# Loads and gradient stores issued by SyncE instead of GpSimd, beside a long zero fill

## The chip, the cores and the metric

The kernel runs on one NeuronCore of a Trainium2 chip. The metric is device time in microseconds of one execution, as a median over runs. The engines are TensorE (PE), VectorE (DVE), ScalarE (ACT), GpSimd (POOL) and SyncE (SP). Transfers between the device's memory and the on-chip memory are issued by SP, ACT or POOL, each into a queue of its own, and are carried out by the core's 16 DMA engines.

## What is computed

One decode step of a transformer block for two sequences, forward and backward: layer norm, attention over the last 4096 positions of a key/value cache, a GELU-gated feed-forward layer, and the gradients of all inputs.

```python
B, Sq, D = 2, 1, 512
Hq, Hkv, Sk, Dh = 32, 8, 32768, 128
F = 1792
W = min(4096, max(256, Sk // 4))                       # 4096

def _A_ref(x, k_cache, v_cache, wq, wo):
    q = heads(x @ wq)
    k = jnp.repeat(k_cache[:, :, Sk - W:, :], rep, axis=1)
    v = jnp.repeat(v_cache[:, :, Sk - W:, :], rep, axis=1)
    p = softmax(einsum("bhqd,bhkd->bhqk", q, k) * Dh ** -0.5)
    return heads_back(einsum("bhqk,bhkd->bhqd", p, v)) @ wo

def _B_ref(x, w_gate, w_up, w_down):
    return (gelu(x @ w_gate) * (x @ w_up)) @ w_down

h  = x + _A_ref(layernorm(x), k_cache, v_cache, wq, wo)
h2 = h + _B_ref(layernorm(h), w_gate, w_up, w_down)
# outputs: h2, and the gradients of x, k_cache, v_cache, wq, wo, w_gate, w_up, w_down
```

All tensors are bfloat16. Two facts set the amount of data. The gradients of the two caches have the caches' full shape, 2 x 8 x 32768 x 128, though only the last 4096 positions differ from zero: the other 28672 positions of each of the 32 (tensor, sequence, head) regions must be written with zeros, 7.34 MB each and 234.9 MB in all. And the gradient at the 4096 positions is another 33.6 MB. The loads are the used parts of the caches (33.6 MB) and the weights.

## The kernel before

The on-chip memory is one large byte array `mem`, and `at(off, shape, ...)` gives a tile at a hand-picked offset, so several tensors use the same bytes in turn. A tile of K or V (`Kt[b, g]`, `Vt[b, g]`) is 1 MB: 128 partitions with 32 cache rows each, 8 KB per partition. Loads go by `load_k` (line 148) and `load_v` (line 152).

The program runs these stages: `attention(0)`, `middle(0)`, `score_grads(0)`, `attention(1)`, `middle(1)`, then `score_grads(1)` interleaved with the weight gradients, the gradient of the query projection, and last the gradients of the caches. `attention(b)` goes through the eight K/V heads g. Within it the order of PE, VectorE and ScalarE is written out by hand (`manual_schedule`), with the softmax steps of head g + 1 put between the products of head g. For SP and GpSimd the order is that of the program text all through.

`prefetch(b, g)` is called at the start of head g and issues what later heads need: in the first sequence K and V of head g + 3, then the output projection (g = 5), the gate weights (6), the up weights and the first two K of the second sequence (8); in the second sequence the V and K tiles, each as its place comes free. K has four places in the first sequence, and in the second some heads share a place, so a K load waits until the head that used it is done.

Zeros are written from a tile `zt` of 128 x 2048 bytes of zero. The transfer reads bytes and writes 4-byte elements, so that a row of 2048 bytes in becomes 8 KB out; casting transfers are issued by GpSimd (`zero_rows`, line 114). `zeros(n)` writes the next n columns, a column being 128 such rows or 1 MB, and there are 7 columns to a region. Where a whole region is started at once and its number is in `ZERO_PARTS`, it goes out as five to seven transfers with other numbers of rows, such as `(15, 18)`: 15 rows of 18 x 8 KB.

Before the change almost all transfers are in GpSimd's one queue, and the program text decides their order: a load, some zeros, a load, and so on. SP issues only x, the query weights, the first two K and V tiles, the down weights (twice) and x once more (line 138, before the weight gradients), and stores the gradient of x (line 857). `store` (line 795) writes the gradients of the output projection and of the feed-forward weights, line 873 those of the query weights, line 909 the 16 stores of the cache gradients of 2 MB each (`dKv`, `dVv`); zeros follow each of them. In the last stage VectorE and ScalarE evacuate the products of line 901 through `evac` (lines 91 and 93) into eight staging places, and each place can be used again when its store has landed.

Of the kernel before, what the change touches and what calls it, by code (L numbers as in the profile page):

```python
# [8 lines left out]
F32 = mybir.dt.float32  # L9
U8 = mybir.dt.uint8  # L10
U32 = mybir.dt.uint32
ACT = mybir.ActivationFunctionType
ALU = mybir.AluOpType
# [3 lines left out]
P = 128  # L17
B, D = 2, 512
# [6 lines left out]
F = 1792  # L25
NFR = F // P
NDR = D // P
NOR = (HQ * DH) // P
# [40 lines left out]
def kernel(ctx, tc, A_x, A_k_cache, A_v_cache, A_wq, A_wo, B_x, B_w_gate, B_w_up, B_w_down, grad_out,  # L69
                out_0, out_1, out_2, out_3, out_4, out_5, out_6, out_7, out_8):  # L70
    nc = tc.nc
# [24 lines left out]
    Kv = A_k_cache[:, :, Z:, :].rearrange("b g (p j) d -> p b g j d", p=P)  # L96
    Vv = A_v_cache[:, :, Z:, :].rearrange("b g (p j) d -> p b g j d", p=P)
# [3 lines left out]
    ZE = 2048  # L101
    zt = const.tile([P, ZE], U8)
    zero_regions = [o[b, g, 0:Z, :].rearrange("r d -> (r d)") for o in (out_2, out_3) for b in range(B) for g in range(HKV)]

    ZPK = Z * DH // 2 // ZE

    ZCOLS = ZPK // P
    ZERO_PARTS = {5: ((4, 1), (15, 2), (2, 2), (15, 18), (12, 1), (128, 4), (16, 4)), 15: ((4, 1), (15, 2), (2, 2), (15, 18), (12, 1), (128, 4), (16, 4)), 27: ((3, 16), (15, 2), (3, 4), (15, 18), (12, 2), (128, 4)), 6: ((6, 2), (1, 6), (9, 2), (12, 2), (4, 1), (128, 6), (16, 4)), 7: ((8, 2), (1, 6), (7, 2), (12, 2), (4, 1), (128, 6), (16, 4)), 14: ((9, 2), (1, 6), (6, 2), (12, 2), (4, 1), (128, 6), (16, 4)), 16: ((10, 2), (1, 6), (5, 2), (12, 2), (4, 1), (128, 6), (16, 4)), 17: ((12, 2), (1, 6), (3, 2), (12, 2), (4, 1), (128, 6), (16, 4)), 18: ((13, 2), (1, 6), (2, 2), (12, 2), (4, 1), (128, 6), (16, 4)), 19: ((14, 2), (1, 6), (1, 2), (12, 2), (4, 1), (128, 6), (16, 4))}
    TAIL_ZEROS = (1, 1, 1, 2, 2, 1, 1, 1, 2, 2, 1, 1, 1, 2, 2, 0)
    z_cols = [0]  # L110

    def zero_rows(dst, rows, n):
        src = zt[0:rows * (P // rows):P // rows, :]
        nc.gpsimd.dma_start(out=dst.rearrange("(p k e) -> p k e", p=rows, k=n),  # L114
                            in_=src.unsqueeze(1).to_broadcast([rows, n, ZE]))

    def zeros(n):
        while n:
            i, c = divmod(z_cols[0], ZCOLS)
            parts = ZERO_PARTS[i] if c == 0 and n >= ZCOLS and i in ZERO_PARTS else ((P, min(n, ZCOLS - c)),)  # L120
            done = c * P
            for rows, k in parts:
                zero_rows(zero_regions[i].bitcast(F32)[done * ZE:(done + rows * k) * ZE], rows, k)
                done += rows * k
            assert done % P == 0
            z_cols[0] += done // P - c
            n -= done // P - c

    dh2_x = at(OFF_XR, [98, D], BF16, "xr")
    dh2_bf, x_32, dh_bf = dh2_x[0:B, :], dh2_x[32:32 + B, :], dh2_x[64:64 + B, :]  # L130
# [10 lines left out]
    wq_sb = at(OFF_WQ, [P, NDR, HQ * DH], BF16, "wq")  # L141
    nc.sync.dma_start(out=wq_sb[:], in_=A_wq.rearrange("(p r) n -> p r n", r=NDR))
    load_rows(nc.scalar)
    Kt, Vt = {}, {}

    def load_k(b, g, eng=nc.gpsimd):
        Kt[b, g] = at(K_OFF[b][g], [P, NJ, DH], BF16, f"K{b}_{g}")
        eng.dma_start(out=Kt[b, g][:], in_=Kv[:, b, g, :, :])

    def load_v(b, g, eng=nc.gpsimd):  # L150
        Vt[b, g] = at(OFF_V + g * 8 * KIB, [P, NJ, DH], BF16, f"V{b}_{g}")
        eng.dma_start(out=Vt[b, g][:], in_=Vv[:, b, g, :, :])

    wo_sb = at(OFF_WO, [P, NOR, D], BF16, "wo")
    wg = at(OFF_WG, [P, NDR, F], BF16, "wg")
    wu = at(OFF_WU, [P, NDR, F], BF16, "wu")
# [5 lines left out]
        nc.sync.dma_start(out=t[:], in_=B_w_down.rearrange("(m r) n -> m r n", r=NFR))  # L162

    def load_wg():
        nc.gpsimd.dma_start(out=wg[:], in_=B_w_gate.rearrange("(p r) f -> p r f", r=NDR))

    def load_wu():
        nc.gpsimd.dma_start(out=wu[:], in_=B_w_up.rearrange("(p r) f -> p r f", r=NDR))

    ident_bf = const.tile([P, P], BF16)  # L170
    nc.gpsimd.memset(ident_bf[:], 0.0)
# [131 lines left out]
    def prefetch(b, g):  # L303
        if b == 0:
            if g == 0:
                load_k(0, 0, nc.sync)
                load_wd(OFF_WD0)
                for i in range(2):
                    load_v(0, i, nc.sync)
                    if i == 0:  # L310
                        load_k(0, 1, nc.sync)
                nc.gpsimd.tensor_scalar(out=zt[:], in0=Kt[0, 0][:, 0:ZE // 256, :].rearrange("p j d -> p (j d)").bitcast(U8),
                                        scalar1=0, scalar2=None, op0=ALU.mult)
                for i in range(2, 4):
                    load_k(0, i)
                    load_v(0, i)
                zeros(9)
            elif g + 3 < HKV:
                load_k(0, g + 3)
                zeros(2)  # L320
                load_v(0, g + 3)
                zeros(2)
            elif g == 5:
                nc.gpsimd.dma_start(out=wo_sb[:], in_=A_wo.rearrange("(p r) n -> p r n", r=NOR))
                zeros(0)
            elif g == 6:
                load_wg()
                zeros(6)
            elif g == HKV:
                load_wu()  # L330
                load_k(1, 0)
                load_k(1, 1)
                zeros(27)
        else:
            if g == 0:
                for i in range(5):
                    load_v(1, i)
                    zeros(1)
                for i in range(2, 5):
                    load_k(1, i)  # L340
                    zeros(1 if i < 4 else 9)
            elif g == 1:
                load_k(1, 5)
                zeros(4)
            elif g == 2:
                load_k(1, 6)
                zeros(5)
            elif g < 6:
                load_v(1, g + 2)
                zeros((5, 5, 2)[g - 3])  # L350
            elif g == 6:
                load_k(1, 7)
                zeros(62)
            elif g == HKV:
                load_wd(OFF_WD)

# [400 lines left out]
    with tc.tile_pool(name="ps_G", bufs=2, space=PSUM) as ps_G:  # L757
# [33 lines left out]
            for k in range(len(n_cols_list)):  # L791
                grad_units.append(unit(k))

        def store(out, in_, n):
            nc.gpsimd.dma_start(out=out, in_=in_)
            zeros(n)

        for (r0, nr, nz) in ((0, 14, 3), (14, 14, 1), (28, 4, 9)):
            add_group([D] * nr, lambda k, r0=r0: Ro_flat[:, (r0 + k)::NOR], lambda k: DH_bf[:],
                      lambda st, r0=r0, nr=nr, nz=nz: store(gwo_v[:, r0:r0 + nr, :],  # L800
                                                            st[:, :nr * D].rearrange("p (a n) -> p a n", n=D), nz))
        row_box = {}

        def rows_from_T(key, srcT_bf):
# [3 lines left out]
            for r in range(NFR):  # L808
                if r == 8:
# [5 lines left out]

        grad_units.append(lambda: rows_from_T("act", actT_bf))
        add_group([D] * NFR, lambda k: row_box["act"][:, k::NFR], lambda k: dh2_bf,
                  lambda st: store(gwd_v, st[:, :NFR * D].rearrange("p (a n) -> p a n", n=D), 8))
        for (key, srcT, o_dram, nz) in (("dg", dgT_bf, out_6, 5), ("du", duT_bf, out_7, 13)):
            grad_units.append(lambda key=key, srcT=srcT: rows_from_T(key, srcT))  # L820
            o_v = o_dram.rearrange("(p r) f -> p r f", r=NDR)
            pieces = [(r, f0, fl) for r in range(NDR) for (f0, fl) in ((0, 512), (512, 512), (1024, 512), (1536, 256))]
            add_group([fl for (_, _, fl) in pieces], lambda k, pieces=pieces: ln2_bf[:, pieces[k][0]::NDR],
                      lambda k, key=key, pieces=pieces: row_box[key][:, pieces[k][1]:pieces[k][1] + pieces[k][2]],
                      lambda st, o_v=o_v, nz=nz: store(o_v, st[:, :NDR * F].rearrange("p (r f) -> p r f", r=NDR), nz))
        g_next = [0]

        def grads(n):
# [7 lines left out]
    with tc.tile_pool(name="ps_W2", bufs=2, space=PSUM) as ps_W, \  # L836
# [27 lines left out]
        for r in range(NDR):  # L864
            st = at(OFF_WQ + r * 8 * KIB, [P, HQ * DH], BF16, "gq")
            for c4 in range(4):
                ps = ps_G.tile([P, 1024], F32, tag="ps_g", name="ps_gq")
                for q in range(2):
                    col0 = c4 * 1024 + q * 512
                    nc.tensor.matmul(out=ps[:, q * 512:(q + 1) * 512], lhsT=L_bf[:, r::NDR],  # L870
                                     rhs=Ro_flat[:, col0:col0 + 512], start=True, stop=True)
                evac(st[:, c4 * 1024:(c4 + 1) * 1024], ps[:])
            nc.gpsimd.dma_start(out=gwq_v[:, r, :], in_=st[:])
            zeros(1 if r < NDR - 1 else 4)

    with tc.tile_pool(name="ps_G3", bufs=3, space=PSUM) as ps_G, \
         tc.tile_pool(name="ps_R", bufs=1, space=PSUM) as ps_R:
# [6 lines left out]
            rowsb = rows4_from_T(ps_R.tile([P, DH], BF16, tag="rows", name="ps_rows")[:], src, f"{n}")  # L884
            return build_bd(OFF_BD + n * 8 * KIB, rowsb[:], f"bd{n}")
        nxt = bd_of(0)
        tail_zeros = list(TAIL_ZEROS)
        for n, (b, what) in enumerate(jobs):
            rhs_bd = nxt
            lhs_bf, dst_v = (ds_bf[b], dKv) if what else (p_bf[b], dVv)  # L890
            for gq in range(2):
# [15 lines left out]
                for a in range(2):  # L907
                    g0 = gq * 4 + a * 2
                    nc.gpsimd.dma_start(out=dst_v[:, b, g0:g0 + 2, :, :], in_=sts[a][:])
                    zeros(tail_zeros.pop(0))  # L910
                if gq == 0 and n + 1 < len(jobs):
                    nxt = bd_of(n + 1)

# [26 lines left out]
```

## Time and profile before

| | us |
|---|---|
| Median of 3 runs (range) | 800.18 (800.13 to 800.91) |
| The profiled execution | 800.13 |
| Its span | 798.4 |
| PE, VectorE, ScalarE, GpSimd busy | 577.7, 474.5, 286.3, 126.0 |

The span is the time from the first to the last instruction; the profiled execution's own time has 1.7 us around it. "Busy" is the sum of an engine's instructions. The waits of the engines, in order of their sums, begin like this (engine, line, what it waited for: us in total, times, longest):

```profile
POOL out_dram L114 <- DMA out_dram<-zt: 258.2, 48, 16.5
PEld L901 <- issue: 102.1, 159, 12.2
ACT mem L394 <- PE KT_ps L392: 60.5, 59, 6.9
...
POOL mem L148 <- DVE mem L443: 48.4, 3, 28.0
POOL out_dram L909 <- DMA out_dram<-mem: 45.5, 11, 4.8
POOL mem L148 <- PE oPK_ps L454: 43.9, 4, 15.7
```

The first line is GpSimd waiting, ahead of a zero fill, for an earlier zero fill to land. The lines with L148 are GpSimd waiting, ahead of a K load, for the compute engines to give the place free.

In the rest of the text "q0" is the queue that GpSimd feeds and "q1" the one that SP feeds, as the profile numbers them.

### The profile page before, as it was taken

The numbers are of one execution on the slowest core, as the hardware profiler recorded it, in microseconds if no ns is written. First come the engines' busy times: TensorE is split into PE (matmuls) and PEld (weight loads), VectorE is DVE, ScalarE is ACT, GpSimd is POOL, SyncE is SP. The second block draws the span as 40 slices with busy tenths as digits, with TensorE's granted clock in tenths as the row PEclk, the third lists the DMA queues.
The fourth block names the chain that finished last, engine by engine and source line by source line (L and its number), as shares of the span: only waits on it lengthen the run. The fifth ranks groups of instructions, "written<-read, shape, count | busy, mean of one in ns | idle before, by whom it ended". The sixth has DMA issues, their size and how long they took to land.

```text
span 798.4 us, 12599 instructions
## 1 busy us (share of the span) xinstructions
PE 577.7 (72%) x5108; PEld 305.3 (38%) x5108; DVE 474.5 (59%) x1160; ACT 286.3 (36%) x410; POOL 126.0 (16%) x210
## 2 busy tenths in 40 slices
PE   3899999887686897998787798978864734756000
PEld 3655554455554554544455444423311211212000
DVE  2369999327533696896426757554589934757000
ACT  1633331135244332312125255543433733646000
POOL 3211210222121000121222221010000121111100
PEclk9999999977797898998968588555957877879555
DMA  8999999999999999999999999999999999999996
GB/s 368 414 426 425 423 433 420 424 428 425 426 426 424 427 419 426 377 325 427 428 423 424 427 429 426 430 428 431 427 429 426 428 428 427 428 428 427 428 430 241
DMA packets 42994, 332.44 MB, mean 416 GB/s; under 512 B 4012, under 2 KB 4024, under 8 KB 4152
## 3 DMA queue, kind: packets, MB, share of 16 engines
q0 software_dynamic: 41904, 319.57, 104.8%
q1 hardware_dynamic: 1020, 12.07, 4.1%
q8 instruction: 40, 0.66, 0.3%
q10 hardware_dynamic: 12, 0.01, 0.1%
q14 instruction: 18, 0.15, 0.0%
HBM read 49.29 MB, written 282.33 MB: 415 GB/s over the span
## 4 chain that ended last, share of the span: by engine, by line
PE 33%; DVE 20%; DMA 19%; ACT 4%; issue 3%; POOL 0%; POOLq 0%; ACTq 0%; DVEq 0%
DMA out_dram<-mem 16%; DVE mem L443 7%; PE M_ps L458 4%; PE ps_tb L251 4%; PE ps_gr L786 4%; PE VT_ps L715 3%; DVE junk L659 3%; PE dP_ps L724 3%; DMA out_dram<-zt 3%; ACT mem L93 2%; PE d_ln_ps L644 2%; DVE mem L282 2%; DVE mem L91 2%; PE attn_ps L589 2%; PE gu_ps L601 2%
## 5 line engine op out<-in xcount | busy, mean ns | idle before, releaser
L443 DVE TENSOR_TENSOR mem<-mem,ee 128x512 bf16<-128x512 bf16 x512 | 178.9, 414 | 30.8 <-PE M_ps L458 30.7
L458 PE MATMUL M_ps<-mem 128*128 128x512 bf16 x512 | 141.1, 400 | 7.5 <-DVE mem L443 2.7
L114 POOL DMA_DIRECT2D out_dram<-zt x133 | 84.9, 666 | 283.6 <-DMA out_dram<-zt 258.2
L901 PE MATMUL ps_g<-mem 128*128 128x512 bf16 x256 | 83.3, 432 | 58.6 <-ACT mem L93 56.0
L91 DVE CAST mem<-ps_g 128x512 bf16<-128x512 f32 x128 | 82.6, 687 | 45.6 <-PE ps_g L901 36.6
L93 ACT CAST mem<-ps_g 128x512 bf16<-128x512 f32 x128 | 73.9, 587 | 72.0 <-DMA out_dram<-mem 37.2
L394 ACT COPY mem<-KT_ps 128x1024 bf16<-128x1024 bf16 x64 | 64.5, 1012 | 60.6 <-PE KT_ps L392 60.5
L901 PEld LDWEIGHTS <-mem 128*128 128x128 bf16 x256 | 27.2, 107 | 115.1 <-issue 102.1
L458 PEld LDWEIGHTS <-mem 128*128 128x128 bf16 x512 | 44.1, 100 | 55.8 <-issue 13.1
L251 PE MATMUL ps_tb<-ident_bf,mem 128*128 128x128 bf16 x480 | 55.9, 250 | 5.5 <-ACT mem L255 1.4
L724 PE MATMUL dP_ps<-mem 128*128 128x512 bf16 x128 | 46.5, 444 | 4.8 <-ACT mem L93 4.8
L251 PEld LDWEIGHTS <-mem 128*128 128x128 bf16 x480 | 37.4, 129 | 31.2 <-issue 29.8
L715 PE MATMUL VT_ps<-ident_bf,mem 128*128 128x128 bf16 x512 | 47.2, 240 | 2.3 <-ACT mem L93 1.1
L93 ACT COPY mem<-VT_ps 128x1024 bf16<-128x1024 bf16 x33 | 33.7, 1021 | 37.9 <-PE VT_ps L715 37.7
L715 PEld LDWEIGHTS <-mem 128*128 128x128 bf16 x512 | 36.8, 107 | 27.3 <-issue 19.7
L392 PE MATMUL KT_ps<-ident_bf,mem 128*128 128x128 bf16 x512 | 43.1, 235 | 1.6 <-DMA out_dram<-zt 1.6
L93 ACT COPY mem<-ps_tb 128x512 bf16<-128x512 bf16 x44 | 25.8, 586 | 51.0 <-PE ps_tb L251 38.1
L91 DVE CAST mem<-ps_gr 128x512 bf16<-128x512 f32 (+1 forms) x40 | 26.7, 670 | 28.8 <-PE ps_gr L786 28.8
L91 DVE COPY mem<-ps_tb 128x512 bf16<-128x512 bf16 x44 | 18.6, 424 | 41.2 <-PE ps_tb L251 38.6
L786 PE MATMUL ps_gr<-mem 2*128 2x512 bf16 (+1 forms) x78 | 33.8, 509 | 11.3 <-DVE mem L810 7.2
L392 PEld LDWEIGHTS <-mem 128*128 128x128 bf16 x512 | 36.9, 108 | 12.4 <-issue 2.5
L454 PE MATMUL oPK_ps<-mem 128*4 128x128 bf16 x1024 | 37.4, 224 | 4.5 <-issue 4.1
(256 smaller groups left out, 627.9 us busy)
## 6 DMA issues: line engine op xcount, KB each, us to landing
out_dram<-zt POOLq DMA_DIRECT2D x8, 6144.0 KB, 31.6
out_dram<-zt POOLq DMA_DIRECT2D x18, 2048.0 KB, 27.0
out_dram<-zt POOLq DMA_DIRECT2D x8, 4096.0 KB, 29.6
out_dram<-mem POOLq DMA_DIRECT2D x16, 2048.0 KB, 33.7
out_dram<-zt POOLq DMA_DIRECT2D x4, 7168.0 KB, 44.0
out_dram<-zt POOLq DMA_DIRECT2D x25, 1024.0 KB, 24.5
out_dram<-zt POOLq DMA_DIRECT2D x8, 3072.0 KB, 32.2
out_dram<-zt POOLq DMA_DIRECT2D x3, 5120.0 KB, 29.6
```

Source lines behind the costliest of these rows:

```text
L91: nc.vector.tensor_copy(out=out, in_=in_)
L93: nc.scalar.copy(out=out, in_=in_)
L114: nc.gpsimd.dma_start(out=dst.rearrange("(p k e) -> p k e", p=rows, k=n), in_=src.unsqueeze(1).to_broadcast([rows, n, ZE]))
L251: nc.tensor.transpose(out=ps[:, a, :], in_=src_block(a), identity=ident_bf[:])
L392: nc.tensor.transpose(out=KT_ps[:, jj, :], in_=Kt[b, g][:, u * 8 + jj, :], identity=ident_bf[:])
L394: nc.scalar.copy(out=KT[:], in_=KT_ps[:])
L443: nc.vector.tensor_tensor(out=pk[:, :, i, :].rearrange("p j (d t) -> p j d t", t=2), in0=Kt[b, g][:, j0:j0 + pk_j, :].rearrange("p j (d t) ...
L458: nc.tensor.matmul(out=M_ps[:], lhsT=Vt[b, g][:, j, :], rhs=pk[:, jj, :, :].rearrange("p i d -> p (i d)"), start=(j == 0), stop=(j == NJ - 1))
L715: nc.tensor.transpose(out=VT_ps[:, jj, :], in_=Vt[b, g][:, a * 8 + jj, :], identity=ident_bf[:])
L724: nc.tensor.matmul(out=dP_ps[:, c, :], lhsT=dOpad[:, w0:w0 + P], rhs=VT[:, c * 4:(c + 1) * 4, :].rearrange("d a k -> d (a k)"), start=(i = ...
L786: nc.tensor.matmul(out=ps[:, :n], lhsT=lhsT_fn(k), rhs=rhs_fn(k), start=True, stop=True)
L901: nc.tensor.matmul(out=ps[:, a2, :], lhsT=lhs_bf[:, jp * P:(jp + 1) * P], rhs=rhs_bd[:, ap * 2 + a2, gq * 4:(gq + 1) * 4, :].rearrange("q ...
```

## The change

Every load of K, V and of the weights, and every store of a weight gradient, is issued by SP. GpSimd keeps the zeros and the 16 stores of the cache gradients. The loads stand in the same order as before among themselves. The zeros are no longer placed between them: at the first `prefetch` GpSimd gets 29 of the 32 regions in one go, and the last three are cut into 15 pieces of 1, 1, 1, 2 and 2 MB that follow the stores of the last stage, one each. `ZERO_PARTS` has three uneven regions (8, 16, 24) in place of ten. The tile `zt` is made from the query weights (times 0) instead of the first K tile.

```diff
-    ZERO_PARTS = {5: ((4, 1), (15, 2), (2, 2), (15, 18), (12, 1), (128, 4), (16, 4)), 15: ...
-    TAIL_ZEROS = (1, 1, 1, 2, 2, 1, 1, 1, 2, 2, 1, 1, 1, 2, 2, 0)
...
+    ZERO_PARTS = {8: ((4, 1), (15, 2), (2, 2), (15, 14), (12, 2), (P, 4), (16, 7)), 16: ((4, 1), (15, 2), (2, 2), (15, 14), (12, 2), (P, 4), (16, 7)), 24: ((3, 16), (15, 2), (3, 4), (15, 18), (12, 2), (P, 4))}
+    ZERO_FIRST, ZERO_CUTS = 29, (1, 1, 1, 2, 2)
+
+    def zero_cast(i):
+        dst, done = zero_regions[i].bitcast(F32), 0
+        for rows, n in ZERO_PARTS.get(i, ((P, ZPK // P),)):
+            src = zt[0:rows * (P // rows):P // rows, :]
+            nc.gpsimd.dma_start(out=dst[done * ZE:(done + rows * n) * ZE].rearrange("(p k e) -> p k e", p=rows, k=n),
+                                in_=src.unsqueeze(1).to_broadcast([rows, n, ZE]))
+            done += rows * n
...
+    def zero_next():
+        if zero_pieces:
+            dst = zero_pieces.pop(0)
+            nc.gpsimd.dma_start(out=dst, in_=zt[:].unsqueeze(1).to_broadcast([P, dst.shape[1], ZE]))
...
-    def load_k(b, g, eng=nc.gpsimd):
+    def load_k(b, g):
         Kt[b, g] = at(K_OFF[b][g], [P, NJ, DH], BF16, f"K{b}_{g}")
-        eng.dma_start(out=Kt[b, g][:], in_=Kv[:, b, g, :, :])
+        nc.sync.dma_start(out=Kt[b, g][:], in_=Kv[:, b, g, :, :])
...
             if g == 0:
-                load_k(0, 0, nc.sync)
+                load_k(0, 0)
                 load_wd(OFF_WD0)
-                for i in range(2):
-                    load_v(0, i, nc.sync)
-                    if i == 0:
-                        load_k(0, 1, nc.sync)
-                nc.gpsimd.tensor_scalar(out=zt[:], in0=Kt[0, 0][:, 0:ZE // 256, :].rearrange("p j d -> p (j d)").bitcast(U8),
-                                        scalar1=0, scalar2=None, op0=ALU.mult)
-                for i in range(2, 4):
+                load_v(0, 0)
+                for i in range(1, 4):
                     load_k(0, i)
                     load_v(0, i)
-                zeros(9)
+                nc.gpsimd.tensor_scalar(out=zt[:], in0=wq_sb[:, 0, 0:ZE // 2].bitcast(U8),
+                                        scalar1=0, scalar2=None, op0=ALU.mult)
+                for i in range(ZERO_FIRST):
+                    zero_cast(i)
             elif g + 3 < HKV:
                 load_k(0, g + 3)
-                zeros(2)
                 load_v(0, g + 3)
-                zeros(2)
...
             elif g == 6:
                 load_k(1, 7)
-                zeros(62)
...
-            nc.gpsimd.dma_start(out=gwq_v[:, r, :], in_=st[:])
-            zeros(1 if r < NDR - 1 else 4)
+            nc.sync.dma_start(out=gwq_v[:, r, :], in_=st[:])
...
                     nc.gpsimd.dma_start(out=dst_v[:, b, g0:g0 + 2, :, :], in_=sts[a][:])
-                    zeros(tail_zeros.pop(0))
+                    zero_next()
```

`load_v`, `load_wg`, `load_wu`, the load of `wo` and the stores that went through `store` change in the same way as `load_k`: `nc.gpsimd` becomes `nc.sync`, and the `zeros(...)` behind them go.

## The prediction

> **What bounds the kernel now.** I read the page's DMA rows first, because the engine rows rule the engines out: PE is busy 72% of the span, VectorE 59%, both in stages with holes.
>
> ```profile
> DMA  8999999999999999999999999999999999999996
> GB/s 368 414 426 425 423 433 420 424 428 425 426 426 424 427 419 426 377 325 427 428 423 424 427 429 426 430 428 431 427 429 426 428 428 427 428 428 427 428 430 241
> DMA packets 42994, 332.44 MB, mean 416 GB/s; under 512 B 4012, under 2 KB 4024, under 8 KB 4152
> ...
> q0 software_dynamic: 41904, 319.57, 104.8%
> q1 hardware_dynamic: 1020, 12.07, 4.1%
> ```
>
> Each GB/s figure is one fortieth of the span, 20 us. Nearly all of them sit at 424 to 430. q0 is GpSimd's queue and q1 is SP's. 332.44 MB at 428 GB/s take 776.7 us, and the span is 798.4, so only 21.7 us are lost, and the change moves no byte more or less. I then cut the span into stretches to find the loss (columns: the stretch, its length, busy time of PE, weight loads, VectorE, ScalarE and GpSimd with counts, PE clock, DMA share, GB/s).
>
> ```profile
> 0.00:10.00 10.00, 0.76 (x12) 0.57 (x12) 4.11 (x20) 1.58 (x2) 2.72 (x19) 1.00 0.80 315
> ...
> 320.00:330.00 10.00, 8.42 (x121) 5.16 (x119) 7.64 (x23) 3.81 (x5) 2.04 (x3) 1.00 0.98 329
> 330.00:340.00 10.00, 9.65 (x119) 5.55 (x118) 9.93 (x34) 3.42 (x5) 1.24 (x2) 1.00 1.14 424
> 340.00:350.00 10.00, 8.68 (x101) 4.13 (x100) 9.28 (x32) 1.83 (x3) 0.00 (x0) 1.00 1.10 412
> 350.00:360.00 10.00, 9.40 (x98) 4.70 (x96) 10.00 (x31) 0.88 (x2) 5.52 (x9) 1.00 0.72 240
> ```
>
> A stretch's loss is its length times the shortfall from 428, over 428. The start loses 10 x 113/428 = 2.6 us. Two dips in the second attention lose 2.3 + 0.4 + 4.4 = 7.1 us. The end is 785 to 798.4:
>
> ```profile
> 785.00:790.00 5.00, 0.00 (x0) 0.00 (x0) 0.00 (x0) 0.00 (x0) 0.00 (x0) 0.50 0.80 324
> 790.00:793.00 3.00, 0.00 (x0) 0.00 (x0) 0.00 (x0) 0.00 (x0) 0.00 (x0) 0.50 0.27 115
> 793.00:795.00 2.00, 0.00 (x0) 0.00 (x0) 0.00 (x0) 0.00 (x0) 0.00 (x0) 0.50 0.06 25
> 795.00:798.40 3.40, 0.00 (x0) 0.00 (x0) 0.00 (x0) 0.00 (x0) 0.00 (x0) 0.50 0.00 0
> ```
>
> That is 1.2 + 2.2 + 1.9 + 3.4 = 8.7 us; a share of 0.06 is one DMA engine of 16 still at work. The remaining 3.3 us are spread thinly. So I price the change only by what it does to the filling and the rate of the DMA engines.
>
> **Part 1: the dips go.** GpSimd issues its queue in order, so a load that waits for a buffer holds every zero fill behind it:
>
> ```profile
> 351.66 0.55 POOL L148 DMA_DIRECT2D mem<-in_A_k_cache_dram  x1 [12.30 <-PE oPK_ps L454]
> ```
>
> The bracket is GpSimd's idle time ahead of the load and what ended it. This wait, and one of 19.05 us that ends at 324.63 for a V load, sit on the dips: the backlog ran out while GpSimd waited. In the changed kernel these waits are SP's; GpSimd has 29 regions of 7.34 MB queued from about 20 us and never waits for a compute engine before its first dK/dV store. The gain is 7.1 us (bounds: 0 if something else drains the queue, 7.1 since no more is lost there). What is late next is the load, not the fill.
>
> **Part 2: the issues.** SP takes over 41 issues (28 K/V, wo, gate, up, ten gradient stores); its own cost 0.25 to 0.63 us each, so at most 26 us of an otherwise idle queue. GpSimd drops from 133 zero issues to 62 (26 whole regions, three cut in seven, 15 tail pieces). Neither engine's issue time is on the path, since transfers stay queued behind it; without that cover the most would be SP's 26 us. Behind a waiting load on SP stand only later loads and stores; their order is that of GpSimd before. zt's source, the query weights instead of K, lets zeros start when the weights land at 13.6 us rather than at 16.2: worth nothing, since SP's loads alone hold 422 GB/s from 10 to 20 us.
>
> **Part 3: two queues busy at once.** Before, SP's queue is nearly alone until 24 us and then carries one 1.8 MB weight load in the middle of zero fills. That load is the best look at the new regime:
>
> ```profile
> 381.67 0.33 SPq L162 DMA_DIRECT2D mem<-in_B_w_down_dram  x1
> ```
> ```profile
> q1 hardware_dynamic: 46, 0.66, 83.0%
> q0 software_dynamic: 36, 0.29, 35.5%
> ```
> ```profile
> 20.00:40.00 20.00, 16.29 (x198) 12.50 (x196) 7.86 (x24) 12.77 (x15) 5.59 (x7) 1.00 1.03 414
> 370.00:392.00 22.00, 20.31 (x157) 8.98 (x157) 13.72 (x45) 2.46 (x3) 3.89 (x7) 0.88 1.16 428
> 392.00:400.00 8.00, 4.79 (x53) 3.35 (x52) 2.79 (x7) 0.29 (x1) 0.31 (x1) 0.94 1.29 426
> ```
>
> The two queue lines are the stretch 393 to 395. The load is issued at 381.7, its first packets come at 393, eleven us later, and then the queues alternate, 46 packets to 36. So SP's loads get about half the rate, some 214 GB/s. SP will carry 49.3 MB of loads and 13.9 MB of gradient stores; 7.4 MB are through by 20 us, so 55.8 MB / 214 GB/s = 261 us with both queues busy. What that costs in rate the trace brackets: from below, 426 against 428 over the 8 us of that one load (0.04 us for 1.84 MB, hence 1.1 us for 55.8); from above, the 414 of 20 to 40 us, where SP's last K/V loads and GpSimd's first transfers share the engines and reads give way to zeros: 261 x 14/428 = 8.5 us. I take the upper end: its packets are the 8 KB K/V rows that make up most of the new traffic, while the load at 393 has 14 KB rows and fewer alternations, and one transfer is too short to show what 261 us of it do.
>
> The Trainium skill speaks against a gain here: "DMA: Bandwidth & Descriptors", section "Issuing engines are not separate DMA queues", says that transfers started by different engines run on the same 16 DMA engines and interleave, so a second issuer saves issue time only. The trace's 46 to 36 packets agree that they interleave; taken as free of cost, the rule would put 0 for the 8.5 us and the sum at 795.4.
>
> **Part 4: the end.** ZERO_PARTS cuts ten regions into uneven parts before and three after; the tail's stores and pieces (1, 1, 1, 2, 2 MB) are the same. If rows go to the 16 engines in turn, a 15-row part leaves one engine out, and adding up both tables gives one engine 8 more rows of 8 KB than before and others 4 fewer to 7 more. A row takes 8192 B / (428/16 GB/s) = 0.31 us: from -1.2 to +2.4 us at the end, where one engine is last. This is an estimate from the code and the rate. I take +2.4, because the largest single change decides when one engine ends last.
>
> **Part 5: loads that land later.** A K load through SP has 11 us of waiting, 4.9 us for 1.05 MB at half rate and some 3 us to complete (the 1.8 MB load: 19.8 us from issue to landing, less 11, less 5.6 at the 0.66 MB in 2 us above): about 19, against
>
> ```profile
> mem<-in_A_k_cache_dram POOLq DMA_DIRECT2D x14, 1024.0 KB, 15.3
> ```
>
> In the first attention a K load has some 21 us (1.6 steps of 13.2 us), so it just fits. The K of the last head, issued at 351.66, landed in 6.8 us because the queue was nearly empty; it will be 12 us later. All this delays the compute engines by 12 to 30 us. I cost it at nothing, because the tail hides it: the first dK/dV pair is evacuated by 607 us, while the bytes ahead of the tail (332.4 - 33.6 stores - 22.0 zero pieces = 276.9 MB) last until 276.9/428 + 3 = 650 us. Its cover is 43 us; beyond it each us of delay costs one.
>
> **Sum.** Span 798.4 - 7.1 + 8.5 + 2.4 = 802.2 us. The profiled run took 800.13 with this span, 1.7 more, and is 0.05 under the median of 800.18: 803.9, so 804.
>
> **Rivals.** *Mixing is free (faster).* The 426 of 392 to 400 holds throughout and the end is as before: 798.4 - 7.1 + 1.1 + 1.7 = 794. For it: the only zero fill under an SP load hardly slows. Against it: that is one load, and 400 to 410, just after it, runs at 423. *The compute engines fall behind the cover (slower).* If every K load lands 3.5 us after its need, in the last twelve steps of both attentions, that is 12 x 3.5 + 12 for the last head = 54 us of delay against 43 of cover, so the DMA engines idle for 11 us ahead of the tail: 815. It decides from a landing of some 24 us on, 2.6 us late each ((43 - 12)/12), and each us more costs 12. For it: the landing has 2 us of room, and each step inherits the delay of the one before. Against it: 19 us is what the one comparable load suggests. *The change does not do what its words say.* The fixed order of attention and the x rows are untouched by the diff: both kernels write the order by hand and load x twice, so nothing is priced for them. The queue part does what it says.
>
> **How the numbers follow.** Forecast (mixing costs) 0.50, its own range 799 to 809; mixing free 0.32; compute behind 0.13; unlisted 0.05. Reaching to 792 takes in most of the second, to 814 part of the third. A measurement tells about 0.2%, 1.6 us, from no change: below 798.6 lies the second case, 0.32; 798.6 to 801.8 the low edge of the first, 0.11; above it 0.57.
>
> **What would show it.** Right: no GB/s slice between 40 and 600 us under 400, q1 at some 63 MB, but slices with SP traffic at 410 to 420 where 425 stood; K landings of 18 to 21 us; end ragged by a few us more. Wrong: 427 throughout (second case), or a slice well under 400 around 650 us (third).

## The result, and the profile after

The changed kernel takes 792.51 us (792.12 to 792.62, four runs) against 800.25 for the kernel before in the same runs: a ratio of 0.9901, 95% interval 0.9884 to 0.9918. It is 7.7 us faster. The forecast was 804, slower; the time is 1.5 us from that of the first rival ("mixing is free", 794). The profiled execution has a span of 790.6 us, against 798.4.

The page's DMA rows of the changed kernel answer to those shown of before:

```profile
DMA  8999999999999999999999999999999999999997
GB/s 364 419 421 421 419 430 421 423 427 430 426 422 419 424 425 425 423 425 428 428 427 427 429 428 427 425 426 425 428 428 429 422 428 427 427 430 426 428 431 283
DMA packets 41409, 332.43 MB, mean 420 GB/s; under 512 B 2428, under 2 KB 2440, under 8 KB 2568
...
q0 software_dynamic: 34416, 268.44, 88.5%
q1 hardware_dynamic: 6924, 63.19, 36.7%
```

The bytes are the same, 63 MB of them are now in SP's queue, and no slice but the first and the last is under 419 GB/s. The two dips are gone. By stretches, the kernel before (columns as in the prediction: stretch, length, busy times, PE clock, DMA share, GB/s):

```profile
320.00:340.00 20.00, 18.07 (x239) 10.71 (x237) 17.57 (x56) 7.23 (x10) 3.28 (x5) 1.00 1.06 376
340.00:360.00 20.00, 18.07 (x197) 8.83 (x195) 19.28 (x61) 2.71 (x5) 5.52 (x9) 1.00 0.91 326
350.00:352.00 2.00, 1.90 (x17) 0.88 (x16) 2.00 (x8) 0.00 (x0) 0.34 (x1) 1.00 0.22 78
```

and the changed kernel, with its end:

```profile
320.00:340.00 20.00, 19.40 (x257) 11.16 (x257) 18.24 (x58) 7.52 (x9) 0.00 (x0) 1.00 1.59 424
340.00:360.00 20.00, 15.48 (x118) 5.93 (x115) 15.80 (x50) 0.90 (x2) 0.53 (x1) 0.83 1.45 425
775.00:780.00 5.00, 0.00 (x0) 0.00 (x0) 0.00 (x0) 0.00 (x0) 0.00 (x0) 0.50 1.06 415
780.00:785.00 5.00, 0.00 (x0) 0.00 (x0) 0.00 (x0) 0.00 (x0) 0.00 (x0) 0.50 0.77 315
785.00:790.00 5.00, 0.00 (x0) 0.00 (x0) 0.00 (x0) 0.00 (x0) 0.00 (x0) 0.50 0.10 41
```

With the prediction's rule (length times shortfall from 428 GB/s, over 428) the time lost to an ideal 776.7 us falls into three parts:

| us lost | up to 20 us | from there to 15 us before the end | last 15 us | sum |
|---|---|---|---|---|
| before | 2.8 | 10.2 (7.2 of them at 320 to 360) | 8.7 | 21.7 |
| changed | 3.0 | 4.3 (0.3 of them at 320 to 360) | 6.6 | 13.9 |

Read like this, the filled dips pay for nearly all of the 7.8 us of span, two queues at once cost about one (10.2 - 7.2 = 3.0 against 4.3 - 0.3 = 4.0) and the end gives two. This sum closes, and the experiments show that its largest entry is no cause by itself.

### The profile page after: what moved, and what is told of

Read it like the earlier page. It is cut to its first block, busy times and chain, and to the rows that moved or that the text cites. A ratio compares the mean times of both kernels' runs of the same rounds, so it can differ in the third digit from the quotient of the medians.

```text
span 790.6 us, 12486 instructions
## 1 busy us (share of the span) xinstructions
PE 579.5 (73%) x5108; PEld 306.2 (39%) x5108; DVE 473.7 (60%) x1160; ACT 286.8 (36%) x410; POOL 65.6 (8%) x97
## 4 chain that ended last, share of the span: by engine, by line
PE 39%; DVE 18%; DMA 17%; ACT 7%; issue 3%; POOLq 0%; ACTq 0%; DVEq 0%; SPq 0%
DMA out_dram<-mem 9%; PE M_ps L448 5%; ACT mem L93 5%; DVE mem L433 5%; PE ps_tb L254 4%; DMA mem<-in_B_w_gate_dram 4%; DMA mem<-in_A_k_cache_dram 4%; PE VT_ps L705 4%; PE dP_ps L714 4%; PE ps_gr L776 4%; PE ps_g L885 3%; DVE mem L91 3%; DVE junk L649 3%; PE d_ln_ps L634 2%; PE attn_ps L579 2%
## 5 line engine op out<-in xcount | busy, mean ns | idle before, releaser
L114 POOL DMA_DIRECT2D out_dram<-zt x46 | 37.1, 1099 | 503.3 <-DMA out_dram<-zt 503.0
L382 PE MATMUL KT_ps<-ident_bf,mem 128*128 128x128 bf16 x512 | 43.3, 235 | 23.2 <-DMA mem<-in_A_k_cache_dram 20.3
## 6 DMA issues: line engine op xcount, KB each, us to landing
mem<-in_A_k_cache_dram SPq DMA_DIRECT2D x16, 1024.0 KB, 22.5
```

Of the source, the lines that this page charges most:

```text
L382: nc.tensor.transpose(out=KT_ps[:, jj, :], in_=Kt[b, g][:, u * 8 + jj, :], identity=ident_bf[:])
```

## The experiments

A time below is a median with the ratio to the kernel before, run beside it, and the 95% interval of that ratio. The kernel before scatters between 799.7 and 803.8 us, most of the others by less than 1 us, so steps between two runs are differences of medians, or of spans where that is said.

### Filling the dips alone

First, the kernel before with only the six waiting loads of the second attention moved to SP:

```diff
-                load_k(1, 5)
+                load_k(1, 5, nc.sync)
```

and the same for K of heads 6 and 7 and for V of heads 5 to 7.

> The kernel before, with only the six K and V loads of the second attention that wait for a place (K of heads 5, 6, 7 and V of heads 5, 6, 7) issued by SP; all else stays in GpSimd's queue. Theory (GpSimd was held behind those loads and its backlog ran out): the two dips at 320 to 360 us go, 7 us, median 793 to 794, ratio 0.991 to 0.993, with 1/10 of the moved bytes. Rival (the gain needs all loads and stores off GpSimd's queue, or comes from the end): 799 to 800, ratio 0.998 to 1.000.

799.9 us, 0.9976 (0.9966 to 0.9987). Second, one queue as before, but more zeros ahead of the waiting loads:

```diff
-                zeros((5, 5, 2)[g - 3])
+                zeros((6, 6, 6)[g - 3])
...
-                zeros(62)
+                zeros(56)
```

> The kernel before, one queue as it was, with 18 MB of zeros in place of 12 ahead of the waiting loads of the second attention (and 6 fewer in the stage after; one uneven part moves from region 14 to region 20, its amount kept). Theory: 6 MB are 14.7 us of backlog, more than both dips, so they go without a second queue: 793 to 794; the K of the last head lands some 10 us later than 6.8 us and that costs nothing. Rival (SP's queue is what helps, for instance by earlier landings): 800, or slower by the later landing, 805 to 810.

799.9 us, 0.9974 (0.9965 to 0.9984). Both are 6 to 7 us short of what the theory of the dips expects. (The second run also moves one uneven part from region 14 to 20; the first leaves the table as it was.) The stretches of the second run say why:

```profile
320.00:340.00 20.00, 18.27 (x239) 10.80 (x238) 17.55 (x56) 7.48 (x10) 3.83 (x6) 1.00 1.13 426
340.00:360.00 20.00, 17.51 (x179) 7.88 (x177) 19.29 (x61) 2.52 (x4) 3.84 (x7) 1.00 1.13 427
...
780.00:785.00 5.00, 0.00 (x0) 0.00 (x0) 0.00 (x0) 0.00 (x0) 0.00 (x0) 0.50 0.57 241
785.00:790.00 5.00, 0.00 (x0) 0.00 (x0) 0.00 (x0) 0.00 (x0) 0.00 (x0) 0.50 0.09 33
790.00:795.00 5.00, 0.00 (x0) 0.00 (x0) 0.00 (x0) 0.00 (x0) 0.00 (x0) 0.50 0.06 25
```

The dips are filled, to 426 and 427. Fifteen of the 16 DMA engines finish some 6 us sooner for it: the rate is down to 241 at 780 to 785, where the kernel before still moves 428. But a share of 0.06 is 1/16, one engine, and 25 GB/s are about a sixteenth of 428; that one works on alone until 794.6 us, and in the first run until 794.7; in the kernel before the last packet ends at 794.9. It gained 0.3 us from the filled dips, so in the profiled execution it had hardly been idle in them: even at 350 to 352 the share before was 0.22, more than 1/16. **The span ends with that engine, not with the mean rate.** The theory of the dips falls as an account of the time.

### What sets the last engine: the table of uneven parts

Two runs of the changed kernel, one with the ten-region table of the kernel before, one with none:

```diff
-    ZERO_PARTS = {8: ..., 16: ..., 24: ...}
+    ZERO_PARTS = {5: ..., 15: ..., 27: ..., 6: ..., 7: ..., 14: ..., 16: ..., 17: ..., 18: ..., 19: ...}
```
```diff
-    ZERO_PARTS = {8: ..., 16: ..., 24: ...}
+    ZERO_PARTS = {}
```

> The changed kernel with the ten-region ZERO_PARTS of the kernel before. The end (from the last full-rate slice to the end of the span) lost 8.7 us before and 6.6 after. If the table sets that: 794.5, ratio to the kernel before 0.993. If the end is set by something else, such as loads no longer sharing GpSimd's queue: 792.5, ratio 0.990.

> The changed kernel with ZERO_PARTS empty, every region as 128 rows of 7 x 8 KB. If the uneven parts take load from one DMA engine that is slower, as counting rows in turn suggests (38 rows of 8 KB at 0.31 us fewer on it): that engine ends up to 12 us later, median 800 to 804, with a tail at 27 GB/s. If the parts do nothing: 792.5. If they hurt: below 792.

798.0 us, 0.9950 (0.9937 to 0.9963), and 804.1 us, 1.0032 (1.0021 to 1.0043). So the table of before costs the changed kernel 5.5 us, more than was expected of either side, and having no table 11.6. The end of the run without a table:

```profile
780.00:785.00 5.00, 0.00 (x0) 0.00 (x0) 0.00 (x0) 0.00 (x0) 0.00 (x0) 0.50 0.64 264
785.00:790.00 5.00, 0.00 (x0) 0.00 (x0) 0.00 (x0) 0.00 (x0) 0.00 (x0) 0.50 0.09 39
790.00:795.00 5.00, 0.00 (x0) 0.00 (x0) 0.00 (x0) 0.00 (x0) 0.00 (x0) 0.50 0.07 26
795.00:800.00 5.00, 0.00 (x0) 0.00 (x0) 0.00 (x0) 0.00 (x0) 0.00 (x0) 0.50 0.05 23
```

Fifteen engines are done by about 786 us, as in the changed kernel; the sixteenth moves 25 GB/s by itself for another 13 us. With no uneven parts one engine ends that much later than the rest. Whether it has more to do or is slower at the same work, and which engine it is, no view of the profile says.

### Table and fill together, in one queue

Now the reverse: the kernel before, in its one queue, with the three parts of the changed kernel, first alone and then with the filled dips too.

```diff
-    ZERO_PARTS = {5: ..., 15: ..., 27: ..., 6: ..., 7: ..., ...}
+    ZERO_PARTS = {5: <as 8 in the changed kernel>, 15: <as 16>, 27: <as 24>}
```

> The kernel before with the three uneven parts of the changed kernel (on regions 5, 15 and 27, where the kernel before can use parts) in place of its ten; queues and order untouched. New theory (one DMA engine has more to move than the others and ends last; the table decides how much is taken off it): the run with the table swapped the other way lost 5.2 us at its last packet, so this gains about as much, span 793 to 794, median 795. The dips still cost the other engines, so not all of the 7.8 us. Theory of the dips: 800.

> The run before with, in addition, 18 MB of zeros in place of 12 ahead of the waiting loads of the second attention: one queue, no dips, table of the changed kernel. New theory (table and dips together are the whole gain, the second queue as such is worth nothing): 791.5 to 793, as the changed kernel. If the second queue has a worth of its own: 795 or more.

797.7 us, 0.9964 (0.9950 to 0.9978), and 794.7 us, 0.9923 (0.9909 to 0.9937). In the first, the last packet comes 3.3 us sooner, at 791.6, and now the other fifteen engines, which pay for the dips, are not far ahead; in the second they finish earlier, and one engine is left alone once more. The ends of the two:

```profile
785.00:790.00 5.00, 0.00 (x0) 0.00 (x0) 0.00 (x0) 0.00 (x0) 0.00 (x0) 0.50 0.72 303
790.00:795.00 5.00, 0.00 (x0) 0.00 (x0) 0.00 (x0) 0.00 (x0) 0.00 (x0) 0.50 0.03 13
```
```profile
780.00:785.00 5.00, 0.00 (x0) 0.00 (x0) 0.00 (x0) 0.00 (x0) 0.00 (x0) 0.50 0.52 216
785.00:790.00 5.00, 0.00 (x0) 0.00 (x0) 0.00 (x0) 0.00 (x0) 0.00 (x0) 0.50 0.06 25
```

Together the two edits bring 5.9 of the 7.7 us without any second queue; fill alone brought 1.4 and the table alone 2.9 (by spans 5.4, 0.3 and 3.4), so they are worth more together than one by one. 2.2 us to the changed kernel remain, 2.4 by spans: 1.1 until the last packet (789.6 against 788.5), and 1.3 from there to the end of the span (3.4 against 2.1).

### How the parts act

The changed kernel with one uneven region, with a fourth one cut anew and put first, with a fourth one cut like region 8 and put last, and with the cut that had been put first moved behind the others:

```diff
-    ZERO_PARTS = {8: ..., 16: ..., 24: ...}
+    ZERO_PARTS = {8: ...}                                                     # e11
+    ZERO_PARTS = {4: ((4, 1), (15, 1), (2, 1), (15, 9), (12, 3), (P, 5), (16, 4)), 8: ..., 16: ..., 24: ...}     # e12
+    ZERO_PARTS = {8: ..., 16: ..., 24: ..., 26: <as 8>}                       # e13
+    ZERO_PARTS = {8: ..., 16: ..., 24: ..., 26: <as 4 in e12>}                # e14
```

> The changed kernel with one uneven region (8) in place of three. New theory, counting rows in turn: 11 rows less on one engine than with no table, 3.4 us at 0.31 us each, so 804.1 - 3.4 = 800.7, against 792.5 with three (38 rows, 11.6 us). If the parts act in another way than by rows on one engine, such as by the (3, 16) part of region 24 alone: 804.

> The changed kernel with one more uneven region (4), which by the same count takes 7 rows, 2.1 us, off the same engine and gives the others one each. In the changed kernel one engine is alone for the last 2.5 us before 788.5. New theory, if that is still the same engine: 790.4 to 791. If another engine is last there: 792.5 or up to 0.3 more.

> The changed kernel with a fourth uneven region, 26, cut as regions 8 and 16 are. By counting rows in turn 11 rows, 3.4 us, less on the last engine, 0.7 rows more on each other. In the changed kernel that engine is alone for about 2.5 us, so the others become last: 2 to 2.5 us gained, 790 to 790.5. If another engine is last in the changed kernel: 792.5 to 793.

> The part that made the changed kernel 11 us slower on region 4, moved unchanged to region 26, behind the other three. Theory (where a part begins depends on the rows dealt before it, and this one shifted the deal, so the three after it missed the slow engine): no harm any more, 790 to 793. Rival (the part itself puts load on the slow engine): 803 again.

| | us | ratio | interval |
|---|---|---|---|
| e11, one region | 801.0 | 0.9997 | 0.9988 to 1.0007 |
| e12, new cut on region 4 | 803.8 | 1.0035 | 1.0023 to 1.0048 |
| e13, fourth region last | 790.4 | 0.9870 | 0.9856 to 0.9885 |
| e14, new cut on region 26 | 792.3 | 0.9894 | 0.9879 to 0.9908 |

Counted by dealing rows to 16 engines in turn, region 8 alone takes 11 rows off one engine and the three take 38. Measured from 804.1, these bring 3.1 and 11.6 us, 0.28 and 0.31 us a row; the count and the estimate of 0.31 hold. The fourth region, 11 rows more, brings only 2.1 us, since then the other engines are nearly as late. No engine is left alone for long at the end of that run, whose last packet ends at 786.3:

```profile
780.00:785.00 5.00, 0.00 (x0) 0.00 (x0) 0.00 (x0) 0.00 (x0) 0.00 (x0) 0.50 0.77 318
785.00:790.00 5.00, 0.00 (x0) 0.00 (x0) 0.00 (x0) 0.00 (x0) 0.00 (x0) 0.50 0.09 36
```

e12 was expected to gain or to do nothing and lost 11 us, as if there were no table at all. Moved unchanged behind the others (e14) the same cut does no harm, though it brings nothing of the 2.1 us counted for it either. So it is its place ahead of the other cuts that hurts, not the cut by itself. My reading is that it shifts where the next uneven cut begins; no run shows that directly. It suggested why the table of before is weak, and three more runs asked for it: its three large regions without the seven small ones, its region 5 alone, and region 5's cut put last in the changed kernel.

> The changed kernel with the three large uneven regions of the kernel before (5, 15, 27) without its seven small ones. With all ten it took 798.0. Theory (the small ones, with their parts of one row of 6 x 8 KB, shift the deal so that regions 15 and 27 miss the slow engine): 46 rows less on that engine, so it is no longer last, 790 to 791. Rival (the large parts of before are the worse ones): 797 to 798.

> The changed kernel with region 5 of the table of before alone. Theory (its last cut, 12 rows of 8 KB, leaves the deal shifted, so the 15-row cuts of regions 15 and 27 miss the slow engine): region 5 does all that the three did, 16 rows x 0.31 = 4.9 us off 804.1, 799.2 to 799.6, the same as with the three. Rival (the three do a third each): 802.6.

> The changed kernel with that same cut as a fourth uneven region, 26, last. Theory (the cut takes 16 rows off the last engine, and nothing comes behind it to be shifted): as with the fourth region cut like regions 8 and 16, 790 to 791. Rival (the cut is too weak or acts on another engine): 792.5 or more.

799.6 us, 0.9980 (0.9969 to 0.9991); 799.9 us, 0.9987 (0.9978 to 0.9996); 790.25 us, 0.9865 (0.9850 to 0.9880). My guess that the seven small regions do the harm was wrong: without them the kernel is 1.5 us slower still. Region 5 alone does as much as the three together, so regions 15 and 27 bring nothing behind it, and its own cut works where nothing follows. Its last cut is 12 rows of one 8 KB piece; the cut in e12 has three such single-piece parts. That single pieces move the starting point otherwise than rows in turn would is consistent with all of these runs, but it is an inference: which of them does it was not tried one by one, and the single-piece part that opens regions 8 and 16 does no such harm.

The Trainium skill has a piece that fits in part: "DMA: Bandwidth & Descriptors", section "Why a DMA increments its semaphore by 16 and not by 1", says that a GpSimd transfer that can't be split over all 16 engines goes to consecutive ones, counted on from a cursor that runs from transfer to transfer. That the 803.8 and 792.3 us of one cut depend on its place agrees with such a cursor, but counted by rows it does not give them: the cut of e12 ends where it began (4 + 15 + 2 + 15 + 12 = 48 rows, three rounds of 16), as those of regions 8 and 16 do. Some part must move the cursor by another count than its rows. No view here names the engine of a packet, so this stays open.

### One queue once more

> One queue, no dips, with the three parts of the changed kernel and a fourth on region 18. The run without the fourth took 794.7 with one engine alone for the last 5 us. Theory (the second queue is worth nothing as such): 11 rows less on that engine, 3.4 us, 791 to 791.5, faster than the changed kernel. If the second queue has a worth beyond that engine's load: 794 or more.

The run of e10 with a fourth part on region 18: 791.8 us, 0.9886 (0.9869 to 0.9903). One queue passes the changed kernel (792.5), but not the same number of parts in two queues (790.4). The last packets are 0.7 us apart, 786.9 against 786.3; the rest is again the stretch from the last packet to the end of the span, 3.4 to 3.5 us in all profiled kernels with the loads in GpSimd's queue and 1.4 to 2.8 in those with the loads on SP (e8 left aside). What the program does in it was not found. So 1.4 us between the two medians stay with the second queue, unexplained; the fourth part also stands on another region in each (18 and 26).

### The cover of the late loads

Fewer zeros ahead of the last stage, more in it:

```diff
-    ZERO_FIRST, ZERO_CUTS = 29, (1, 1, 1, 2, 2)
+    ZERO_FIRST, ZERO_CUTS = 27, (2, 2, 3)          # e5
+    ZERO_FIRST, ZERO_CUTS = 25, (3, 4)             # e6
```

> The changed kernel with 27 regions at the start in place of 29 and five regions in 15 pieces of 2, 2 and 3 MB behind the stores of the last stage. Tests the cover of step 5. In the changed kernel GpSimd's first cache-gradient store is issued at 626 us with 11.5 MB ahead of it in its queue, that is 27 us. Two regions less are 14.7 MB or 34 us, so the DMA engines should run dry for about 34 - 27 = 7 us plus some 2 us of start: 800 to 803. If the compute engines hide more than that (or the dry time is filled by SP's stores): 792.5.

> The same with 25 regions at the start and seven regions in 14 pieces of 3 and 4 MB: 68.6 us less cover against 27, so dry for 42 us and some us of start: 832 to 838, slope against the run with 27 regions one us for each us. If the cover argument is wrong: under 800.

798.9 us, 0.9978 (0.9960 to 0.9996), and 834.3 us, 1.0422 (1.0395 to 1.0448). The stretches of the first, then of the second run, where the changed kernel has 425 GB/s from 600 to 640:

```profile
600.00:640.00 40.00, 28.22 (x79) 9.07 (x80) 35.80 (x50) 21.70 (x34) 2.86 (x4) 0.71 0.87 342
```
```profile
560.00:600.00 40.00, 34.42 (x190) 14.05 (x189) 18.59 (x36) 16.22 (x27) 0.00 (x0) 0.76 0.41 162
600.00:640.00 40.00, 28.48 (x76) 9.23 (x77) 34.54 (x48) 20.16 (x31) 2.97 (x4) 0.67 0.55 220
```

The DMA engines run dry for 40 x 86/428 = 8 us in the one and for 25 + 19 = 44 us in the other. Each us of cover that is missing costs about one us, and the cover in the changed kernel is the roughly 27 us of transfers that were still queued when the first cache gradient was ready. e5 is 1 us better than expected; in its profile the last 15 us lose 3.8 us in place of 6.6, as they do in e6, perhaps because the engines start level after the dry time.

### Two queues at once

The cache-gradient stores on SP too (`nc.gpsimd.dma_start` to `nc.sync.dma_start` in the last loop), and K and V loads in four pieces each:

```diff
-        nc.sync.dma_start(out=Kt[b, g][:], in_=Kv[:, b, g, :, :])
+        for c in range(0, NJ, 8):
+            nc.sync.dma_start(out=Kt[b, g][:, c:c + 8, :], in_=Kv[:, b, g, c:c + 8, :])
```

> The changed kernel with the 16 cache-gradient stores issued by SP too, the 15 zero pieces still by GpSimd, so that two queues are busy in the last stage. Theory (two queues at once cost about 1.4 us for 55.8 MB): 33.6 MB more, at most 1 us, 792 to 794; the compute engines wait less, since a store lands sooner. My forecast (414 in place of 428 GB/s while both are busy): zero pieces of 22 MB against as many bytes of stores, 44 MB at 3.3% less, 3.4 us: 796.

> The changed kernel with each K and V load cut into four loads of 8 cache rows per partition, so that its packets have 2 KB in place of 8 and the queues alternate four times as often, 28 x 4 issues more on SP. Theory (alternating is nearly free): under 3 us more, 792 to 796. My forecast's mechanism (rate lost at each change of queue, 8.5 us for the packets of the changed kernel): 4 x the K/V share of that, over 15 us more, 808 or above. A loss by small packets alone, with no part for the queues, would look like the second and could not be told from it by this run.

The first takes 792.5 us, 0.9895 (0.9878 to 0.9912), the same as the changed kernel. Its rate in the last stage, above the changed kernel's for the same stretch:

```profile
680.00:720.00 40.00, 24.27 (x73) 7.97 (x74) 28.93 (x43) 20.85 (x36) 3.67 (x6) 0.84 1.11 421
```
```profile
680.00:720.00 40.00, 25.64 (x83) 8.27 (x82) 27.12 (x43) 23.61 (x41) 5.88 (x9) 0.87 1.07 428
```

Two queues of stores cost 1.6% of the rate here, half of what I had taken, and the 2.1 us that this makes until 15 us before the end come back in the last 15, where 4.4 us are lost in place of 6.6.

The second takes 891.3 us, 1.1132 (1.1110 to 1.1154), and tells nothing of alternation. Its GB/s row, then a line of its waits (who waited for what: us in total, times, longest):

```profile
GB/s 355 404 413 412 413 413 413 413 412 424 417 416 428 427 414 411 414 412 412 412 411 414 421 430 424 429 427 428 363 83 82 83 1 223 392 426 428 428 428 360
```
```profile
PE KT_ps L384 <- DMA mem<-in_A_k_cache_dram: 126.2, 19, 24.5
```

While loads run it moves 412 or 413 GB/s, but what it loses is the gap after slice 28: the zeros are done and the compute engines are not there yet, because TensorE has waited 126 us for K. That is the rival "the compute engines fall behind the cover", brought about by more and smaller loads; why K came so late was not followed up.

## Why the prediction was wrong, point by point

**What bounds the kernel.** "So I price the change only by what it does to the filling and the rate of the DMA engines" was half right. The engines are the bound, but the mean rate over 16 of them is not: the end is that of the last one. I had read the sign of it, "a share of 0.06 is one DMA engine of 16 still at work", and taken it for a ragged edge of 2 us. Two terms of the sum failed as well: part 3 was too large by 7 us or more, and part 4, the price of the last engine, had the wrong sign.

**Part 1, the dips, -7.1.** They went as foreseen (7.2 us lost before, 0.3 after), though the 29 regions were not all queued at once: GpSimd waited 503 us in all for earlier fills to land. By themselves the dips are worth 0.3 us of span, since in that execution the last engine was hardly idle in them, and 1.4 us by the medians (e2; 2.1 by its ratio, 0.9974). These differ because the kernel before scatters from 800.0 to 803.8 us beside e2, which stays within 799.5 to 800.3. The other runs in which the DMA engines run low on the way scatter too (e9 from 796.3 to 801.0, e5 from 796.4 to 801.9); that the dips cause it was not tested. In full they pay only when the last engine is relieved too.

**Part 3, two queues at once, +8.5.** The term was mis-sized, and that alone turns the sign: with 1.1 in place of 8.5 the sum gives a span of 794.8 and a time of 796.5 us. From 20 us to 15 us before the end the changed kernel loses 4.3 us; one-queue kernels without dips lose 2.8 (e10), 4.2 (e16) and 4.8 (e2). So the cost is at most some 1.5 us and can't be told from nothing; the lower bound was 1.1. I chose the upper bound for its 8 KB rows. But in the 414 of 20 to 40 us the two queues were side by side only from 24 to about 30 us, both with loads and at 410 to 426 GB/s, and the lowest rate, 399 at 36 to 40 us, is that of GpSimd's queue alone, about where its loads give way to zeros. The 426 at 392 to 400 was the only case of loads beside zeros. The rule of the Trainium skill that stands beside this term ("DMA: Bandwidth & Descriptors", "Issuing engines are not separate DMA queues"), taken as free of cost, came nearer than my 8.5. e7 shows that the cost isn't always nothing: 421 against 428 GB/s with stores on both.

**Part 4, the end, +2.4.** Wrong in sign and size, and the largest part of the result: with the dips filled, the change's table is better than that of before by 5.2 us in one queue (e2 to e10) and by 5.5 in two (e3). The count of rows in turn was good for the changed table (0.28 to 0.31 us a row) and false for the table of before, which by that count takes 46 rows off one engine and by the runs acts like some 20 (798.0 against 804.1).

**Part 5, the late loads.** Later than I had said, and hidden as I had said. K loads land after 22.5 us, not 19; the one of the last head after 30.8, and TensorE waits 20.3 us for it. Three views of the changed kernel: its issues by size (count, KB, us to landing), its waits, and GpSimd's timeline.

```profile
mem<-in_A_k_cache_dram SPq DMA_DIRECT2D x16, 1024.0 KB, 22.5
```
```profile
PE KT_ps L382 <- DMA mem<-in_A_k_cache_dram: 20.3, 1, 20.3
```
```profile
625.73 0.73 POOL L893 DMA_DIRECT2D out_dram<-mem  x1 [66.22 <-DVE mem L274]
```

The reload of x on SP comes at 469.6 in place of 448.5 us, 21 us late, and the span is 7.8 us shorter. The first cache-gradient store is issued at 625.7; before, its pair was evacuated by 607, so the delay there is 19 us. 9.3 MB of GpSimd's zeros and 2.6 MB of SP's stores were still to move then, some 27 us at 428 GB/s. That is about what 43 us of cover less the delay leave, and e5 and e6 show that it is what hides the delay.

**Part 2, the issues.** At nothing, as priced. (GpSimd's zero issues are 61, not 62: one of the three cut regions has six parts.)

**The rivals.** "Mixing is free" gave 794 and came closest, but by a sum whose terms were partly wrong: 7.1 for the dips, nothing for the table. That it lands near is luck: fifteen engines gain by the dips, and the sixteenth happens to gain about as much by the table (its last packet comes at 788.5 in place of 794.9). "The compute engines fall behind the cover" stayed out, with a landing of 22.5 us under the 24 from which it was to decide.

A version faster than both kernels is the changed kernel with a fourth uneven region behind the other three: 790.25 us (e18) and 790.4 (e13), 1.3% under the kernel before.

## What to carry to other kernels

Where transfers are the bound, look at the last microseconds engine by engine: a DMA share of 1/16 over several us, at a sixteenth of the full rate, was here the sign that one engine sets the time, and then filling holes in the mean rate buys little until work is taken off that engine. Take it off by uneven transfers, one change at a time and the newest one last, because an uneven transfer can undo those that come after it (e12). And of two bounds for an unseen cost, take the row in which the same thing happens, however short, over the row that only looks like it in size.

## What the runs showed that was not expected

- Without uneven parts one of 16 DMA engines ends 13 us after the others in an 800 us kernel that keeps them at 417 to 433 GB/s nearly to the end (e4); the cause was not found.
- The same uneven cut costs 11 us or nothing depending on its place among the others (803.8 in e12, 792.3 in e14).
- A 1 MB load on SP's queue lands after 22.5 us beside a full GpSimd queue, although half of 428 GB/s, an estimate of SP's share, would need 5. The last K load lands after 30.8 us, and TensorE waits 20.3 us for it.
